# Splitting the experts' second weights during the first network instead of during the experts' first pass

## The chip, the cores and the metric

The kernel runs on one core of a Trainium2 chip. The metric is the time of one execution on the device in microseconds (us), taken as the median of several executions; lower is better. A change of 0.2% (2.4 us) is about what a measurement of this kernel can tell from no change.

## The reference

Everything is float32. A linear attention over 2304 tokens is followed by a network with a gated activation (the first network), and that by four experts whose outputs are mixed by probabilities:

```
kv  = einsum('bhsd,bhde->bhse', q, einsum('bhsd,bhse->bhde', k, v))
x   = kv / sqrt(mean(kv*kv) + 1e-6) * g_norm            # (2304, 512)
h   = x @ w_in                                          # w_in (512, 2048)
x   = (h * clip(h + 3, 0, 6) / 6) @ w_out               # w_out (2048, 512)
p   = probs / (sum(probs) + 1e-9)                       # (2304, 4)
out = sum over e of p[:, e] * (relu(x @ w1[e]) @ w2[e]) # w1 (4, 512, 1024), w2 (4, 1024, 512)
```

## The kernel before

Every float32 operand of a matrix product is split into a rounded high part and a low remainder, and a product is three TensorE matmuls (high by high, high by low, low by high). A split is one ScalarE copy (the high part) and one VectorE subtraction (the low part); the helper `split` at L667 and L668 records both.

**Stages.** Attention takes the first 90 us or so. The first network then runs over "items" (u, t, f): 16 hidden tiles of 128 columns in five units u, five token blocks t (four of 512 tokens and one of 256), tile f within the unit. `step(n)` issues the first layer of item n (`ff_in`: 12 matmuls into one of two PSUM banks `ph`), the second layer of item n-3 (`ff_out`: 12 matmuls into `po`), and pieces of `convert`, which loads and splits the weights of a later hidden tile. Between the layers stand ScalarE L371, VectorE L372 (the last reader of `ph`), ScalarE L374 and VectorE L375. When a unit is complete, VectorE L411 adds `po` to `acc`.

**The experts.** Three passes of 768 tokens. An expert's hidden columns are taken 256 at a time, which makes 16 "quads" k. In the first pass `quad(k)` makes seven block products of Strassen's kind with `product` (L821, 6 matmuls each, in turn into the PSUM banks `qa` and `qb`) and brings the results out with ScalarE and VectorE (L856 is ScalarE's copy `us` of the second product; the product that follows two places later writes the same bank). `outs(k-1)` then multiplies by the second weights (L777, 36 matmuls). Beside the matmuls the first pass prepares the weights of the next quads: `convert_in` splits w1 and its block sums into `win` and stores them (L687), `convert_out` splits w2 into `wout`, forms four block differences of w2 on GpSimd (L699, tile `tw`), splits them, and stores the differences and three plain blocks to DRAM (`dtw`, L709 and L711). Passes two and three read `dtw` and the stored `win` back and use Strassen's form for both layers (L1029).

**Order.** Inside the attention the order is written by hand. Behind it a scheduler sets the order on each engine when the program is built; an engine then takes its instructions in that order. All large DMAs are issued by SyncE (SP), which also issues in order and stands still at a DMA whose source or target is not ready.

**Buffers the change touches.** `cvp` holds the four 2 KB-per-partition work tiles of `convert` (x, a and two r), `rawp` three raw weight tiles of 4 KB; both pools end after the first network, and their space is used again by `win`. `tw` lived in `accp`, whose five buffers hold `acc` until the tokens of a pass have been read.

Of the kernel before, what the change touches and what calls it, by code (L numbers as in the profile page):

```python
# [8 lines left out]
F32 = mybir.dt.float32  # L9
F32R = mybir.dt.float32r  # L10
U32 = mybir.dt.uint32
AF = mybir.ActivationFunctionType
ALU = mybir.AluOpType
# [4 lines left out]
def kernel(  # L18
# [18 lines left out]
    nc = tc.nc  # L37
    B, H, S, D = q.shape
    NT, DM = out.shape
    E = moe2_w1.shape[0]  # L40
    P = 128
# [17 lines left out]
    FP = NF2 // 2  # L59
    NW = 8  # L60
    NA = NW - 2
    LAG = 3
    RATE = (4200, 3000, 2600, 2900, 0)
    FMAX = 3.0e38
    PADL, PADR = 232, 248
# [6 lines left out]
    accp = ctx.enter_context(tc.tile_pool(name="accp", bufs=NB))  # L72
# [7 lines left out]
    cvp = early.enter_context(tc.tile_pool(name="cvp", bufs=1, side="right"))  # L80
    rawp = early.enter_context(tc.tile_pool(name="rawp", bufs=3, side="right"))
# [3 lines left out]
    dram = ctx.enter_context(tc.tile_pool(name="dram", bufs=1, space=bass.MemoryType.DRAM))  # L85
    psk = attps.enter_context(tc.tile_pool(name="psk", bufs=1, space=bass.MemoryType.PSUM))
    psp = attps.enter_context(tc.tile_pool(name="psp", bufs=1, space=bass.MemoryType.PSUM))
    NG = CJ * 2
# [25 lines left out]
    ftiles = [(u, f) for u in range(NUNIT) for f in range(UF[u])]  # L114
# [38 lines left out]
    def convert(n):  # L153

        u, f = ftiles[n]
        W[u, f] = w = wp.tile([P, 2, 2, KD * P], F32R, tag=f"w{(NA + n) % NW}", name="w")

        for h in range(2):
            lo, hi = raw[n, h][:, :, 0], raw[n, h][:, :, 1]
            x = cvp.tile([P, KD * P], U32, tag="x", name="x")  # L160
            a = cvp.tile([P, KD * P], U32, tag="a", name="a")
            r = cvp.tile([P, KD * P], F32, tag="r", bufs=2, name="r")
            xf, up = x.bitcast(F32), r.bitcast(U32)
            nc.scalar.activation(out=xf, in_=hi.bitcast(F32), func=AF.Abs)
            nc.scalar.activation(out=up, in_=lo, func=AF.Copy, scale=2.0 ** -29)
            yield 0
            nc.vector.tensor_scalar(
                out=xf, in0=xf, scalar1=2.0 ** -15, scalar2=122880.0, op0=ALU.max, op1=ALU.min)
            yield 335
            nc.vector.tensor_scalar(  # L170
                out=x, in0=x, scalar1=5, scalar2=2,
                op0=ALU.logical_shift_left, op1=ALU.logical_shift_right)
            yield 335
            nc.vector.scalar_tensor_tensor(
                out=a, in0=hi, scalar=0xC0000000, in1=x, op0=ALU.bitwise_and, op1=ALU.bitwise_or)
            yield 600
            e = nc.gpsimd if POOLED[0] <= (n, h) < POOLED[1] else nc.vector
            e.tensor_tensor(out=up, in0=up, in1=a, op=ALU.add)
            yield 600 if e is nc.vector else 0
            nc.scalar.activation(out=w[:, h, 0], in_=r, func=AF.Copy)  # L180
            yield 0
            nc.vector.tensor_tensor(out=w[:, h, 1], in0=r, in1=w[:, h, 0].bitcast(F32), op=ALU.subtract)
            if n:
                load_raw()
            yield 600

# [312 lines left out]
    with tc.manual_schedule(engines=engines):  # L499
# [103 lines left out]
        for y in range(2):  # L603
            h = half[y]
            for jp in range(2):
# [5 lines left out]
                out=prob[h, B * HH:], in0=dp[h, y::2, CJ - 1],  # L611
                in1=psum_e[h, y::2, CJ - 1:].to_broadcast([D, 2, E]), op=ALU.mult)

    N3 = start[NU1 - 1, 0] + 3 * UF[NU1 - 1]
    for n in range(NB, N3 + 1):
        step(n)
    assert cv[0] == len(ftiles)

# [18 lines left out]
    quads = [(0, e, j) for e in range(E) for j in range(FP)]  # L639
    NQ = len(quads)  # L640
    SIDES = NPASS - 1
    TC = DM // 2
    dwin = [dram.tile([P, 2, 7, 2, P], F32, name=f"dwin{k}") for k in range(NQ)]
    dtw = [dram.tile([P, 7, 2, 2, TC], F32, name=f"dtw{g}") for g in range(NQ // 2)]
    dwo = [dram.tile([P, 2, 2, DM], F32, name=f"dwo{k}") for k in range(2)]
    raw2, win, wout, xs, g2, acc2 = {}, {}, {}, {}, {}, {}
    sums = xsp.tile([P, 4, 2, P], F32, tag="sums", name="sums")
    st1 = xsp.tile([P, 2, TH], F32, tag="st1", name="st1")
# [16 lines left out]
    def split(dst, src):  # L665

        nc.scalar.activation(out=dst[0], in_=src, func=AF.Copy)  # L667
        nc.vector.tensor_tensor(out=dst[1], in0=src, in1=dst[0].bitcast(F32), op=ALU.subtract)  # L668
# [21 lines left out]
    def convert_out(k):  # L690

        r = raw2.pop(k)[:, 1].rearrange("p (f d) -> p f d", f=2)
        wout[k] = w = wp.tile(
            [P, 2, 2, DM], F32R, tag=f"w{(NA + len(ftiles) + 2 + k % 2) % NW}", name="wout")
        b11, b12, b21, b22 = (r[:, f, c * TC:(c + 1) * TC] for f in range(2) for c in range(2))
        tw = accp.tile([P, 2, 4, TC], F32R, tag="acc", name="tw")
        ts = tw[:, 1].bitcast(F32)
        for z, a, b in ((0, b12, b11), (1, b22, ts[:, 0]), (2, b22, b12), (3, b21, ts[:, 1])):
            nc.gpsimd.tensor_tensor(out=ts[:, z], in0=a, in1=b, op=ALU.subtract)  # L699
        for f in range(2):  # L700
            split([w[:, f, y] for y in range(2)], r[:, f])
            yield
        for z in (slice(0, 2), slice(2, 4)):
            split([tw[:, y, z] for y in range(2)], ts[:, z])
            if z.start:
                load2(k + 2)
                dt = dtw[k // 2][:, :, k % 2]
                for z, m in enumerate((4, 2, 3, 5)):
                    nc.sync.dma_start(out=dt[:, m], in_=tw[:, :, z].bitcast(F32))  # L709
                for m, f, c in ((0, 0, 0), (1, 1, 0), (6, 1, 1)):  # L710
                    nc.sync.dma_start(out=dt[:, m], in_=w[:, f, :, c * TC:(c + 1) * TC].bitcast(F32))  # L711
                if k >= NQ - 2:
                    nc.sync.dma_start(out=dwo[k - NQ + 2], in_=w.bitcast(F32))
            yield

    def build(p):
# [160 lines left out]
    def run(g):  # L877
        return lambda: next(g, None)
# [24 lines left out]
    for k in range(NQ):  # L903
        last_of_pass = k + 1 == NQ
        ci, co = convert_in(k + 1) if 0 < k and k + 1 < NQ else iter(()), convert_out(k)
        side = rest_in + builds + [run(co)] * 4 + [run(ci)] * (1 if builds else 5)
        rest_in = [run(ci)] * 4 if builds else []
        builds = []
        if last_of_pass:
            nxt = build(1)  # L910
            side += [nxt[1], nxt[0]]
            builds = [nxt[m] for m in (6, 5, 2, 7, 3, 4)]
        seed()
        every = -(-NI2 * 6 // len(side))
        for z, _ in enumerate(filler):
            if z % every == every - 1 and side:
                side.pop(0)()
        for x in side:
            x()
        quad(k)  # L920
        if k + 1 < NQ:
            seed = first_product(k + 1)
        filler = outs(k)
# [16 lines left out]
    def load_t(n):  # L940
        if 2 * n >= 7 * (NG2 - 1):
            return
        tt[n] = t = accp.tile([P, 2, 2, 2, TC], F32R, tag="acc", name="tt")
        for y in range(2):
            g, m = divmod(2 * n + y, 7)
            if g < NG2 - 1:
                nc.sync.dma_start(out=t[:, y].bitcast(F32), in_=dtw[g % (NQ // 2)][:, m])

    def front(g, jj):

# [190 lines left out]
```

## Time and profile before

| | |
|---|---|
| median of 3 runs | 1207.6 us (1207.46 to 1207.98) |
| profiled execution, its own time | 1207.61 us |
| its span, first to last instruction | 1205.8 us |
| TensorE busy | 1182.4 us of the span |
| mean granted TensorE clock | 0.997 |

The span is 1.8 us shorter than the time of the same execution. A matmul's end is modelled in the profile, so places where TensorE stands still are found as idle time with what ended it, and as the distance between the starts of equal pieces of work.

### The profile page before, as it was taken

The page shows a single profiled execution, that of the slowest core. Times are in us where ns is not written, and L with a number is a line of the kernel's source. Part 1 is how long each engine was busy: PE and PEld are TensorE (multiplying, and loading weights), DVE is VectorE, ACT ScalarE, POOL GpSimd, SP SyncE. Part 2 cuts the span into 40 slices and gives each one's busy share as a digit, 9 for nine tenths or more (in the row PEclk, how much of TensorE's full clock was granted, in tenths as well). Part 3 has the DMA queues.
Part 4 walks back from the last instruction along what each step waited for, and adds up shares of the span by engine and source line. Part 5 has one row for each costly group of instructions (what it writes and reads, how often), then busy time and mean ns, then how long its engine had stood idle before and what let it go on. Part 6 is the DMA issues. An engine that isn't in the chain of part 4 may idle for free.

```text
span 1205.8 us, 19484 instructions
## 1 busy us (share of the span) xinstructions
PE 1182.4 (98%) x7810; PEld 1076.4 (89%) x7810; DVE 766.1 (64%) x1380; ACT 561.2 (47%) x1020; POOL 55.8 (5%) x79
## 2 busy tenths in 40 slices
PE   8999999999999999999999999999999999999998
PEld 7788888888888889888888889999999999999997
DVE  5889994833433765565757565666666866666663
ACT  6876553522322445455555434444444544444442
POOL 1100000000000022211111000000000000000000
PEclk9999999999999999999999999999999999999999
DMA  9723330200200237788888866667666887666641
GB/s 319 230 87 105 103 107 2 86 1 1 71 1 1 123 97 247 286 291 303 282 281 283 336 235 230 250 245 249 245 249 244 300 279 266 241 253 246 248 171 53
DMA packets 87278, 230.45 MB, mean 191 GB/s; under 512 B 7188, under 2 KB 52244, under 8 KB 80532
## 3 DMA queue, kind: packets, MB, share of 16 engines
q1 hardware_dynamic: 86704, 228.43, 53.8%
q8 instruction: 61, 1.00, 0.3%
q10 hardware_dynamic: 484, 0.79, 0.2%
q14 instruction: 29, 0.24, 0.1%
HBM read 163.65 MB, written 65.54 MB: 190 GB/s over the span
## 4 chain that ended last, share of the span: by engine, by line
PE 73%; DVE 8%; ACT 7%; DMA 6%; POOL 2%; issue 2%; SPq 2%; POOLq 0%; DVEq 0%; ACTq 0%
PE slot L1029 16%; PE po L393 14%; PE qb L821 11%; PE qa L821 10%; PE ph L358 5%; PE ph L360 5%; PE ph L359 5%; PE po L777 4%; DMA dtw<-tw 3%; POOL tw L699 2%; ACT so L667 2%; DMA dwin<-win 1%; PE slot L1106 1%; ACT ar L958 1%; DVE sums L1006 1%
## 5 line engine op out<-in xcount | busy, mean ns | idle before, releaser
L1029 PE MATMUL slot<-tt,so 128*128 128x256 f32 x1890 | 248.6, 283 | 3.0 <-ACT so L667 1.4
L1029 PEld LDWEIGHTS slot<-tt,so 128*128 128x128 f32 x1890 | 240.3, 190 | 7.0 <-ACT slot L1037 4.6
L821 PE MATMUL qb<-xs,win 128*128 128x384 f32 x1008 | 204.4, 337 | 4.8 <-ACT us L856 3.8
L821 PE MATMUL qa<-xs,win 128*128 128x384 f32 x1008 | 204.7, 337 | 3.9 <-ACT us L856 3.0
L393 PE MATMUL po<-gH,w 128*128 128x512 f32 (+1 forms) x632 | 191.6, 368 | 0.6 <-DVE acc L411 0.3
L821 PEld LDWEIGHTS qb<-xs,win 128*128 128x128 f32 x1008 | 177.1, 189 | 8.1 <-ACT us L856 6.1
L821 PEld LDWEIGHTS qa<-xs,win 128*128 128x128 f32 x1008 | 173.1, 189 | 6.8 <-ACT us L856 4.4
L794 DVE SCALAR_TENSOR_TENSOR acc<-slot,prob,acc 128x256 f32<-128x256 f32 (+1 forms) x252 | 108.1, 484 | 106.4 <-PE slot L1029 96.5
L393 PEld LDWEIGHTS po<-gH,w 128*128 128x128 f32 x632 | 115.8, 188 | 21.1 <-DVE acc L411 0.8
L777 PE MATMUL po<-wout,g 128*128 128x512 f32 x576 | 133.8, 390 | 0.0
L777 PEld LDWEIGHTS po<-wout,g 128*128 128x128 f32 x576 | 107.9, 188 | 21.9
L358 PE MATMUL ph<-xh,w 128*128 128x512 f32 (+1 forms) x320 | 118.6, 371 | 0.0
L359 PE MATMUL ph<-xl,w 128*128 128x512 f32 (+1 forms) x320 | 117.9, 368 | 0.0
L360 PE MATMUL ph<-xh,w 128*128 128x512 f32 (+1 forms) x320 | 117.8, 368 | 0.0
L371 ACT ACTIVATE r<-ph,three 128x512 f32<-128x512 f32 (+1 forms) x80 | 51.3, 641 | 141.3 <-PE ph L360 140.4
L372 DVE SCALAR_TENSOR_TENSOR r<-r,ph 128x512 f32<-128x512 f32 (+1 forms) x80 | 50.5, 632 | 104.6 <-ACT r L371 104.6
L393 PE MATMUL po<-gL,w 128*128 128x512 f32 (+1 forms) x316 | 116.4, 368 | 0.0
L668 DVE TENSOR_TENSOR so<-ar,so 128x768 fp32r<-128x768 f32 x94 | 89.4, 952 | 36.5 <-ACT so L667 36.4
L667 ACT ACTIVATE so<-ar 128x768 fp32r<-128x768 f32 x94 | 79.3, 844 | 38.1 <-PE slot L1029 33.5
L958 ACT ACTIVATE ar<-cs 128x384 f32<-128x384 f32 x64 | 33.4, 521 | 80.9 <-DVE cs L987 48.2
L358 PEld LDWEIGHTS ph<-xh,w 128*128 128x128 f32 x320 | 60.3, 188 | 10.7 <-DVE r L372 0.4
L360 PEld LDWEIGHTS ph<-xh,w 128*128 128x128 f32 x320 | 60.3, 188 | 10.1
(160 smaller groups left out, 1335.3 us busy)
## 6 DMA issues: line engine op xcount, KB each, us to landing
win<-dwin SPq DMA_DIRECT2D x32, 1792.0 KB, 8.1
tt<-dtw SPq DMA_DIRECT2D x105, 512.0 KB, 5.8
dwin<-win SPq DMA_DIRECT2D x16, 1792.0 KB, 6.4
raw<-in_moe_w_dram SPq DMA_DIRECT2D x32, 512.0 KB, 4.8
dtw<-tw SPq DMA_DIRECT2D x64, 256.0 KB, 6.0
dtw<-wout SPq DMA_DIRECT2D x48, 256.0 KB, 6.0
raw<-in_moe_w_in_dram SPq DMA_DIRECT2D x14, 512.0 KB, 3.7
raw<-in_moe_w_out_dram SPq DMA_DIRECT2D x14, 512.0 KB, 3.7
```

Source lines behind the costliest of these rows:

```text
L358: nc.tensor.matmul(ph, lhsT=w[:, 0, c, :], rhs=xH[t][:, c, :], start=(c == 0), stop=False)
L359: nc.tensor.matmul(ph, lhsT=w[:, 0, c, :], rhs=xL[t][:, c, :], start=False, stop=False)
L360: nc.tensor.matmul(ph, lhsT=w[:, 1, c, :], rhs=xH[t][:, c, :], start=False, stop=(c == KD - 1))
L371: lambda: nc.scalar.activation(out=r, in_=ph, func=AF.Relu, bias=three[:, 0:1]),
L372: lambda: nc.vector.scalar_tensor_tensor(out=r, in0=r, scalar=6.0, in1=ph, op0=ALU.min, op1=ALU.mult),
L393: nc.tensor.matmul(po_t[u, t][o], lhsT=lhsT, rhs=rhs, start=(f == 0 and m == 0), stop=(f == UF[u] - 1 and m == 2))
L667: nc.scalar.activation(out=dst[0], in_=src, func=AF.Copy)
L668: nc.vector.tensor_tensor(out=dst[1], in0=src, in1=dst[0].bitcast(F32), op=ALU.subtract)
L777: nc.tensor.matmul(ps[i], lhsT=lhsT, rhs=w[:, f, y], start=(j == 0 and f == 0 and m == 0), stop=(j == FP - 1 and f == 1 and m == 2))
L794: nc.vector.scalar_tensor_tensor(out=acc2[i][:, c], in0=ps, scalar=pe, in1=acc2[i][:, c], op0=ALU.mult, op1=ALU.add)
L821: nc.tensor.matmul(bank, lhsT=w[:, wy, AOP[m], c], rhs=xs[m][:, xy, c], start=first and n == 0, stop=n == 5, skip_group_check=True)
L1029: nc.tensor.matmul(dst, lhsT=o[:, sy_, jj, i * P:(i + 1) * P], rhs=t[:, jj, ty], start=fresh and m == 0 and i != 1, stop=m == 5, skip_grou ...
```

## The change

The formation of the block differences and the whole of `dtw` and `dwo` (the plain w2 of the last two quads, read by the very last group) move out of `convert_out` into a new generator `blocks`, which runs during the first network. It loads w2 a second time into `rawp` (L626 of the new file, 512 KB a quad), forms the differences on VectorE (L654 to L659; GpSimd has no part in it any more), splits differences and plain blocks with ScalarE (L644) and VectorE (L645) into the four `cvp` tiles, and stores high and low parts apart (L648, L650). It runs in two stretches, quads 0 to 7 and quads 8 to 15, called from `second(n)` after `step(n)`. For that the conversion of the last two hidden tiles of the first network is held back: their raw tiles are loaded only at n = 48 and 49. `convert_out` keeps the two splits of `wout` and the load of the quad after next. The order of the seven blocks in `dtw` is another one, and the reader follows it.

```
+    HELD = 13
@@ convert
-            if n:
+            if n and n != HELD:
                 load_raw()
@@ new, behind the attention and ahead of the loop over step(n)
+    def load_rawt(k):
+        e, j = experts[k]
+        f = 2 * j * P
+        rawt[k] = r = rawp.tile([P, 2, DM], F32, tag="raw", name="rawt")
+        nc.sync.dma_start(out=r, in_=moe2_w2[e, f:f + 2 * P, :].rearrange("(f p) d -> p f d", p=P))
+    def blocks(k, end, deep):
+        r = rawt[k].rearrange("p f (c d) -> p (f c) d", c=2)
+        last = k - 2 * NG + 2
+        def new():
+            tag = ("x", "a", "r", "r")[turns[0] % 4]
+            turns[0] += 1
+            return cvp.tile([P, 2, TC], F32R, tag=tag, bufs=2 if tag == "r" else 1, name="tb")
+        def keep(m, src, low, n=2):
+            high = new()
+            low = low if low is not None else new()
+            src = low.bitcast(F32) if src is None else src
+            nc.scalar.activation(out=high[:, :n], in_=src, func=AF.Copy)
+            nc.vector.tensor_tensor(out=low[:, :n], in0=src, in1=high[:, :n].bitcast(F32), op=ALU.subtract)
+            for y, x in ((0, high), (1, low)):
+                c = min(n, 7 - m) if m else 1
+                nc.sync.dma_start(out=dtw[k // 2][:, m:m + c, k % 2, y], in_=x[:, :c].bitcast(F32))
+                if last >= 0 and m < 2:
+                    nc.sync.dma_start(
+                        out=dwo[last][:, int(m > 0), y].rearrange("p (c d) -> p c d", c=2), in_=x.bitcast(F32))
+        odd = new()
+        nc.vector.tensor_tensor(out=odd.bitcast(F32), in0=r[:, 1::2], in1=r[:, 0:2], op=ALU.subtract)
+        yield
+        even = new()
+        ev = even.bitcast(F32)
+        nc.vector.tensor_tensor(out=ev[:, 0], in0=r[:, 3], in1=odd[:, 0].bitcast(F32), op=ALU.subtract)
+        nc.vector.tensor_tensor(out=ev[:, 1], in0=r[:, 2], in1=ev[:, 0], op=ALU.subtract)
+        yield
+        keep(3, None, odd)
+        yield
+        keep(5, None, even)
+        yield
+        keep(1, r[:, 2:4], None)
+        yield
+        if last >= 0:
+            keep(0, r[:, 0:2], None)
+        else:
+            keep(0, r[:, 0:1], None, 1)
+        rawt.pop(k)
+        if k + deep < end:
+            load_rawt(k + deep)
+        yield
+    def second(n):
+        if n == 37:
+            for k in range(2):
+                load_rawt(k)
+            stream.extend(x for k in range(NG) for x in [blocks(k, NG, 2)] * 6)
+        elif n == 54:
+            for k in range(NG, NG + 3):
+                load_rawt(k)
+            stream.extend(x for k in range(NG, 2 * NG) for x in [blocks(k, 2 * NG, 3)] * 6)
+        for _ in range(5 if 37 < n < 48 else 4 if 54 < n < 68 else 0):
+            if stream:
+                next(stream.pop(0))
+        if n in (48, 49):
+            load_raw()
     for n in range(NB, N3 + 1):
         step(n)
+        second(n)
@@ convert_out
-        tw = accp.tile([P, 2, 4, TC], F32R, tag="acc", name="tw")
-        ts = tw[:, 1].bitcast(F32)
-        for z, a, b in ((0, b12, b11), (1, b22, ts[:, 0]), (2, b22, b12), (3, b21, ts[:, 1])):
-            nc.gpsimd.tensor_tensor(out=ts[:, z], in0=a, in1=b, op=ALU.subtract)
         for f in range(2):
             split([w[:, f, y] for y in range(2)], r[:, f])
-            yield
-        for z in (slice(0, 2), slice(2, 4)):
-            split([tw[:, y, z] for y in range(2)], ts[:, z])
-            if z.start:
+            if f == 1:
                 load2(k + 2)
-                dt = dtw[k // 2][:, :, k % 2]
-                for z, m in enumerate((4, 2, 3, 5)):
-                    nc.sync.dma_start(out=dt[:, m], in_=tw[:, :, z].bitcast(F32))
-                for m, f, c in ((0, 0, 0), (1, 1, 0), (6, 1, 1)):
-                    nc.sync.dma_start(out=dt[:, m], in_=w[:, f, :, c * TC:(c + 1) * TC].bitcast(F32))
-                if k >= NQ - 2:
-                    nc.sync.dma_start(out=dwo[k - NQ + 2], in_=w.bitcast(F32))
             yield
@@ the loop over quads
-        side = rest_in + builds + [run(co)] * 4 + [run(ci)] * (1 if builds else 5)
+        side = rest_in + builds + [run(co)] * 2 + [run(ci)] * (1 if builds else 5)
@@ load_t, passes two and three
-                nc.sync.dma_start(out=t[:, y].bitcast(F32), in_=dtw[g % (NQ // 2)][:, m])
+                nc.sync.dma_start(out=t[:, y].bitcast(F32), in_=dtw[g % NG][:, (0, 1, 5, 4, 3, 6, 2)[m]])
```

TensorE's order is the same in both programs, matmul for matmul. The order moves at three places on the engines beside it.

First, ScalarE in the experts' first pass, at the end of quad 2's products and the beginning of quad 3's; `raw_4831` is the raw tile of quad 4. Before:

```order
L833 ACTIVATE qb<-qa 128x384
L667 ACTIVATE win<-sums 128x512 x2
L667 ACTIVATE tw<-tw 128x512 x2
L667 ACTIVATE wout<-raw_4831 128x512 x2
L856 ACTIVATE us<-qa 128x384
```

The same place now, where `raw_5258` is the raw tile of quad 4:

```order
L897 ACTIVATE qa<-qb 128x384
L746 ACTIVATE win<-sums 128x512 x2
L746 ACTIVATE wout<-raw_5258 128x512 x2
L920 ACTIVATE us<-qa 128x384
L922 ACTIVATE sums<-qb 128x384
```

The two copies of `tw` ahead of `wout` and `us` are gone, and nothing has come in their place.

Second, VectorE in the first stretch, at items 41 and 42 of the first network (each begins with the instruction that reads `ph`). Before:

```order
L372 SCALAR_TENSOR_TENSOR r<-r,ph 128x512
L375 TENSOR_TENSOR gL<-r,gH 128x512
L372 SCALAR_TENSOR_TENSOR r<-r,ph 128x512
L375 TENSOR_TENSOR gL<-r,gH 128x512
```

The same two items now:

```order
L373 SCALAR_TENSOR_TENSOR r<-r,ph 128x512
L376 TENSOR_TENSOR gL<-r,gH 128x512
L658 TENSOR_TENSOR tb<-rawt,tb 128x256
L659 TENSOR_TENSOR tb<-rawt,tb 128x256
L645 TENSOR_TENSOR tb<-tb 128x512 x2
L373 SCALAR_TENSOR_TENSOR r<-r,ph 128x512
L645 TENSOR_TENSOR tb<-rawt,tb 128x256
L376 TENSOR_TENSOR gL<-r,gH 128x512
L645 TENSOR_TENSOR tb<-rawt,tb 128x512
L654 TENSOR_TENSOR tb<-rawt 128x512
L658 TENSOR_TENSOR tb<-rawt,tb 128x256
```

One quad's blocks are spread over two items, and they stand between the two instructions that each item needs.

Third, VectorE at items 49 and 50, between the stretches, where the held hidden tiles are converted. Before:

```order
L372 SCALAR_TENSOR_TENSOR r<-r,ph 128x256
L375 TENSOR_TENSOR gL<-r,gH 128x256
L182 TENSOR_TENSOR w<-r,w 128x512 x2
L178 ISA r<-r,a 128x1024
L174 SCALAR_TENSOR_TENSOR a<-raw,x 128x512
L178 ISA r<-r,a 128x1024
L372 SCALAR_TENSOR_TENSOR r<-r,ph 128x512
L182 TENSOR_TENSOR w<-r,w 128x512 x2
L375 TENSOR_TENSOR gL<-r,gH 128x512
```

The same two items now:

```order
L373 SCALAR_TENSOR_TENSOR r<-r,ph 128x256
L376 TENSOR_TENSOR gL<-r,gH 128x256
L168 TENSOR_SCALAR x<-x 128x512
L171 TENSOR_SCALAR x<-x 128x512
L175 SCALAR_TENSOR_TENSOR a<-raw,x 128x512
L179 ISA r<-r,a 128x1024
L373 SCALAR_TENSOR_TENSOR r<-r,ph 128x512
L168 TENSOR_SCALAR x<-x 128x512
L183 TENSOR_TENSOR w<-r,w 128x512
L171 TENSOR_SCALAR x<-x 128x512
L376 TENSOR_TENSOR gL<-r,gH 128x512
L175 SCALAR_TENSOR_TENSOR a<-raw,x 128x512
```

Most of this conversion was done by item 36 before; now all of it stands at items 49 to 53, and the first blocks of the second stretch follow at item 53.

## Rows read from the trace of the kernel before

**Rows 1.** Page, parts 1 and 2: busy time; DMA share in 40 slices.
```profile
PE 1182.4 (98%) x7810; PEld 1076.4 (89%) x7810; DVE 766.1 (64%) x1380; ACT 561.2 (47%) x1020; POOL 55.8 (5%) x79
...
DMA  9723330200200237788888866667666887666641
```
**Rows 2.** Windows: stretch, length, then busy us of each engine, clock, DMA share, GB/s.
```profile
90.00:420.00 330.00, 329.98 (x1556) 277.08 (x1555) 206.56 (x373) 134.71 (x224) 0.00 (x0) 1.00 0.17 54
241.00:256.00 15.00, 15.00 (x68) 12.43 (x67) 4.15 (x6) 3.48 (x6) 0.00 (x0) 1.00 0.00 1
440.00:710.00 270.00, 262.22 (x1337) 235.75 (x1336) 165.46 (x311) 139.53 (x278) 42.43 (x58) 0.99 0.78 274
492.50:495.90 3.40, 3.40 (x11) 3.40 (x12) 1.37 (x3) 1.27 (x3) 0.00 (x0) 0.50 0.75 221
```
**Rows 3.** Waits, all engines, 430 to 730 us: total, times, longest.
```profile
POOL tw L699 <- DMA dtw<-tw: 145.8, 11, 19.2
...
ACT win L667 <- DVE sums L680: 11.5, 13, 1.1
...
PE qb L821 <- ACT us L856: 3.8, 4, 2.1
...
PE qa L821 <- ACT us L856: 3.0, 3, 1.8
```
**Rows 4.** Timeline of ScalarE, 472 to 512 us: start, length, instruction, idle before.
```profile
489.51 0.63 ACT L667 ACTIVATE tw<-tw 128x512 fp32r<-128x512 f32 x1 [6.39 <-POOL tw L699]
...
491.91 0.47 ACT L856 ACTIVATE us<-qb 128x384 f32<-128x384 f32 x1
...
507.73 1.15 ACT L667 ACTIVATE wout<-raw 128x512 fp32r<-128x512 f32 x2 [0.88 <-PE po L777]
508.79 0.49 ACT L856 ACTIVATE us<-qa 128x384 f32<-128x384 f32 x1
```
**Rows 5.** Timeline of GpSimd, 440 to 560 us.
```profile
487.35 1.43 POOL L699 TENSOR_TENSOR tw<-raw 128x256 f32<-128x256 f32 x2 [19.25 <-DMA dtw<-tw]
```
**Rows 6.** Timeline of TensorE, 463 to 716 us: starts of the blocks of `outs`.
```profile
464.28 8.36 PE L777 MATMUL po<-wout,g 128*128 128x512 f32 x36
479.82 8.36 PE L777 MATMUL po<-wout,g 128*128 128x512 f32 x36
...
693.39 8.36 PE L777 MATMUL po<-wout,g 128*128 128x512 f32 x36
```
**Rows 7.** Tile `tw`: instructions with ns min/median/max, and its stores' us to landing.
```profile
L667 ACT ACTIVATE tw<-tw x32: 616/632/636, 432.3 to 670.4; 128x512 fp32r<-128x512 f32 x32
L668 DVE TENSOR_TENSOR tw<-tw x32: 683/692/694, 433.1 to 671.1; 128x512 fp32r<-128x512 f32 x32
...
DMA to landing us min/median/max: 2.1/6.0/8.3
```
**Rows 8.** Groups by form, 90 to 440 us: busy us, mean ns, idle before.
```profile
L371 ACT ACTIVATE r<-ph,three 128x512 f32<-128x512 f32 x59 | 40.5, 686 | 118.5 <-PE ph L360 117.6 <-DVE w L182 0.8
...
L375 DVE TENSOR_TENSOR gL<-r,gH 128x256 fp32r<-128x256 f32 x11 | 4.6, 421 | 2.9 <-ACT gH L374 2.9
L374 ACT ACTIVATE gH<-r 128x256 fp32r<-128x256 f32 x11 | 4.6, 418 | 5.7 <-DVE r L372 5.7
```
**Rows 9.** Chain that ended last, 240 to 300 us: start, length, blocks of `ff_out`.
```profile
240.41 2.72 PE po L393 x12
245.85 2.72 PE po L393 x12
...
288.09 2.75 PE po L393 x12
292.27 2.75 PE po L393 x12
```
**Rows 10.** Page, part 6: DMAs, count, KB each, median us to landing.
```profile
dtw<-tw SPq DMA_DIRECT2D x64, 256.0 KB, 6.0
...
raw<-in_moe_w_in_dram SPq DMA_DIRECT2D x14, 512.0 KB, 3.7
```

More of the change, by code (lines that the diff above doesn't have):

```diff
@@ L612 @@
                 in1=psum_e[h, y::2, CJ - 1:].to_broadcast([D, 2, E]), op=ALU.mult)
+    TC = DM // 2
+    experts = [(e, j) for e in range(E) for j in range(FP)]
+    NG = len(experts) // 2
+    dtw = [dram.tile([P, 7, 2, 2, TC], F32, name=f"dtw{g}") for g in range(NG)]
+    dwo = [dram.tile([P, 2, 2, DM], F32, name=f"dwo{k}") for k in range(2)]
+    rawt = {}
+    def load_rawt(k):
[3 more added lines that the diff above has]
+        nc.sync.dma_start(out=r, in_=moe2_w2[e, f:f + 2 * P, :].rearrange("(f p) d -> p f d", p=P))
@@ new lines @@
+    turns = [0]
+    def blocks(k, end, deep):
[39 more added lines that the diff above has]
+        yield
@@ new lines @@
+    stream = []
+    def second(n):
+        if n == 37:
+            assert todo[0] == (HELD + 1, 1) and cv[0] == HELD + 1
+            for k in range(2):
+                load_rawt(k)
+            stream.extend(x for k in range(NG) for x in [blocks(k, NG, 2)] * 6)
+        elif n == 54:
+            assert not stream and cv[0] == len(ftiles)
+            for k in range(NG, NG + 3):
[6 more added lines that the diff above has]
+            load_raw()
@@ L616 @@
         step(n)
-    assert cv[0] == len(ftiles)
+        second(n)
+    assert not stream
     early.close()
@@ L641 @@
     SIDES = NPASS - 1
-    TC = DM // 2
     dwin = [dram.tile([P, 2, 7, 2, P], F32, name=f"dwin{k}") for k in range(NQ)]
-    dtw = [dram.tile([P, 7, 2, 2, TC], F32, name=f"dtw{g}") for g in range(NQ // 2)]
-    dwo = [dram.tile([P, 2, 2, DM], F32, name=f"dwo{k}") for k in range(2)]
     raw2, win, wout, xs, g2, acc2 = {}, {}, {}, {}, {}, {}
@@ L694, in convert_out @@
             [P, 2, 2, DM], F32R, tag=f"w{(NA + len(ftiles) + 2 + k % 2) % NW}", name="wout")
-        b11, b12, b21, b22 = (r[:, f, c * TC:(c + 1) * TC] for f in range(2) for c in range(2))
-        tw = accp.tile([P, 2, 4, TC], F32R, tag="acc", name="tw")
-        ts = tw[:, 1].bitcast(F32)
-        for z, a, b in ((0, b12, b11), (1, b22, ts[:, 0]), (2, b22, b12), (3, b21, ts[:, 1])):
-            nc.gpsimd.tensor_tensor(out=ts[:, z], in0=a, in1=b, op=ALU.subtract)
         for f in range(2):
             split([w[:, f, y] for y in range(2)], r[:, f])
-            yield
-        for z in (slice(0, 2), slice(2, 4)):
-            split([tw[:, y, z] for y in range(2)], ts[:, z])
-            if z.start:
+            if f == 1:
                 load2(k + 2)
-                dt = dtw[k // 2][:, :, k % 2]
-                for z, m in enumerate((4, 2, 3, 5)):
-                    nc.sync.dma_start(out=dt[:, m], in_=tw[:, :, z].bitcast(F32))
-                for m, f, c in ((0, 0, 0), (1, 1, 0), (6, 1, 1)):
-                    nc.sync.dma_start(out=dt[:, m], in_=w[:, f, :, c * TC:(c + 1) * TC].bitcast(F32))
-                if k >= NQ - 2:
-                    nc.sync.dma_start(out=dwo[k - NQ + 2], in_=w.bitcast(F32))
             yield
```

## The prediction

> **What bounds the kernel now.** I read the page first: TensorE is busy 1182.4 of 1205.8 us [rows 1], so only its idle time and its slow stretches can be won. Then the windows, for the two stages that the change touches [rows 2]. In the first network TensorE works 329.98 of 330 us; nothing can be won there, only lost. VectorE works 206.6 us of these and ScalarE 134.7, but in 241 to 256 us, where no weights are converted, they work 4.15 and 3.48 of 15 us and DMA does nothing. In the first expert pass TensorE works 262.2 of 270 us at clock 0.99, so 7.8 us are idle, and DMA is busy at 0.78 with 274 GB/s.
>
> The waits say who ends that idle time: TensorE's two largest entries are products that wait for ScalarE's copy `us`, 3.8 us in 4 places and 3.0 in 3, longest 2.1 [rows 3]. ScalarE is busy about half of the stretch, so I followed one such place back in the timelines. `us` starts at 491.91 us, behind a copy of `tw` at 489.51 that had waited 6.39 us for GpSimd [rows 4]; GpSimd's subtraction at 487.35 had stood 19.25 us until a store of the `tw` before it had landed [rows 5]. Such waits for stores add up to 145.8 us [rows 3], a store taking 6.0 us at the median [rows 7]. So the chain is store, GpSimd, ScalarE in its fixed order, TensorE. Behind the stall the granted clock is 0.50 for 3.4 us (1.2 instead of 2.4 GHz) [rows 2], half of which, 1.7 us, is lost.
>
> **What the change removes.** The chain as a whole: ScalarE's order has no `tw` left ahead of `us`, and nothing waits on GpSimd. What a quad takes without the chain I read from the starts of the `outs` blocks: 464.28 to 479.82 is 15.54 us, a quad without a stall. From 464.28 to 693.39 are 14 quads in 229.11 us, where 14 times 15.54 makes 217.56. The difference, **11.55 us** [rows 6], holds idle time and slow clock together, and it is the term of the gain. Are 15.54 us within reach of every quad? At 507.73 a quad without a stall already shows the order that all will have: `wout` starts when TensorE's `outs` ends, and `us` follows at 508.79 [rows 4], which TensorE did not have to wait for. The 32 copies of `tw` on ScalarE (0.632 us, 20.2 in all) and 32 subtractions on VectorE (0.692 us, 22.1) [rows 7] also go; they lie beside matmuls, and as work they count nothing.
>
> **What it adds, and what hides it.** A quad's blocks cost VectorE four instructions of 0.69 us and three 256-wide ones of 0.42 us, together 4.0 us, and ScalarE three of 0.63 and one of 0.42, 2.3 us (512-wide forms as in [rows 7], 256-wide as in [rows 8]). For 16 quads that is 64 us of VectorE and 37 us of ScalarE. By the order a quad is spread over two items; an item of 512 tokens takes 245.85 - 240.41 = 5.44 us, and a short one 292.27 - 288.09 = 4.18 us [rows 9]. So VectorE gets 4.0 us more in 10.88 us, on top of 4.15 in 15 us: under 0.7 busy. In sum this fits; what matters is whether an instruction that waits holds up the two that each item needs, since both engines work in order.
>
> Slack of these two: `ph` has two banks, so the VectorE instruction that empties it may end as late as the first layer of the item after next, three blocks of 2.72 us on. Less ScalarE's copy and VectorE's own instruction (0.69 each) [rows 8], some 6.8 us are left; where two of the three blocks are 256 wide, 1.43 us each (4.18 - 2.75), 5.6 - 1.4 = some 4 us.
>
> Now the wait. A block tile is formed, its low part split, stored, written again as another block's high part, stored again, once per quad. That loop is 0.69 + 0.63 + 0.69 + 0.63 = 2.64 us and two stores. No row shows such a store on idle queues; its bounds are the 2.1 us minimum and the 6.0 us median among the crowd of the first pass [rows 7]. With 2.1 the loop is 6.9 us, well inside 10.88, and the added cost is **0**. With 6.0 it is 14.6 us, 3.8 more than two items allow: 16 quads fall 60 us behind, of which each of the two stretches absorbs its slack of 6.8, and some **47 us** are lost. It decides at a store of (10.88 - 2.64) / 2 = 4.1 us. I take a value near the lower bound: the network moves 54 GB/s now [rows 2], and the change adds, per two items, 8 stores of 256 KB and a load of 512 KB, 2.6 MB in 10.88 us or 240 GB/s, below the 274 of the first pass, in single pairs of stores and not in the seven at once that `tw` was followed by. A 512 KB load took 3.7 us where the network loads now [rows 10], and that is twice a store's size.
>
> ScalarE and VectorE take their instructions in order, as `us` at 491.91 shows, which did not pass the copies in front of it [rows 4]. The Trainium skill, "TensorE: Matmul & The Clock Gate", section "Architectural detail: the array is 16× 32×32, not 1× 128×128", says that these two engines' queues are strictly first in, first out; by that rule a late store holds the network's own instructions too, which is the slower rival below. The Trainium skill, "DMA: Bandwidth & Descriptors", section "Anatomy of one DMA — SWDGE (gpsimd) path", gives some 2.0 us fixed plus the bytes at 436 GB/s; that is 2.6 us for 256 KB, for a path that this kernel's stores do not take, and the loop would be 7.8 us: also inside two items, and the sum stays. No row settles it, since the fastest store of this trace took 2.1 us.
>
> The held conversion: items 46 to 52 last 6 x 4.18 + 5.44 = 30.5 us, and at items 49 to 53 VectorE has four half tiles to convert, five instructions each, beside its own work and L411. Counted from the order that is nearly all of the 30 us, so VectorE can fall 2 to 3 us behind there; slack is 4 to 6.8 us. I put it at 0, with 3 as the upper bound. The same goes for the end, where the last quad's blocks meet the preparation of the experts (items 67 on): 0, at most 3. Stores of the pass move to where DMA is idle; the first pass loses 112 stores, and what loads remain can only come sooner. Passes two and three keep their work and reads.
>
> **Sum.** 1207.6 - 11.6 + 0 = **1196.0 us**; the profiled execution's own time is 1207.61, that of the runs too, so nothing is to be converted.
>
> **The rivals.**
> *A part is eaten.* Either the network stalls 3 to 6 us (the two upper bounds just named), or in the first pass another wait takes the chain's place. For the second speaks that ScalarE already waits 11.5 us in 13 places for `sums` [rows 3], which is in front of `wout` and `us` in the order now; 0.4 us at each of 15 quads would be 6 us. Against it speaks the quad at 507.73, which has that order and no stall. 1198.5 to 1205.2 us.
> *It moves nothing.* The stall costs as much at another place: the gain of 11.6 us is matched by as much in the network, as when a store takes (11.6 + 13.6) / 32 = 0.8 us more than the deciding 4.1. Within 2.4 us of before, 1205.2 to 1210 us.
> *Slower.* Stores land in more than 5.0 us on the mean: TensorE waits in 270 to 400 us on `ph` or on gH and gL, each quad costs up to 3.8 us, and each stall also brings 1.2 GHz behind it, as at 492.5. Up to 47 us: 1210 to 1243. For it speaks the 6.0 us median, against it the idle queues (slices 9 to 14 of the DMA line, 241 to 422 us, read 002002 [rows 1]).
>
> **How the numbers follow.** The forecast, 1193.5 to 1198.5, gets 0.66; a part eaten, up to 1205.2, 0.16; nothing moved 0.07; slower 0.11. A measurement tells about 0.2%, 2.4 us, from no change. So faster is 0.82, same 0.07, slower 0.11. The range has to leave out 2 in 10 at most: from 1193.5 (a little of the quad ahead of 464 us and of the load on DMA may also be won) to 1205.0 it holds the first two cases.
>
> **What would show it.** Right: in the first pass no product waits for `us`, the `outs` blocks start 15.5 us apart throughout, and the clock stays at 1.0; GpSimd is idle; in 260 to 400 us VectorE is busy about 0.7 or more, TensorE still without a gap, and block stores land in 2 to 4 us. Wrong in size: the blocks are 15.9 us apart, or products wait for `us` behind `wout` or `sums`. Wrong in sign: ScalarE's copies of blocks wait for DMA, and first-layer matmuls wait for L372 (now L373), or the second stretch's items come late on their `w`.

## The result and the profile after

The changed kernel takes 1195.99 us (median of 4 runs, 1194.90 to 1198.16) against 1207.66 us, a ratio of 0.9905 (95% interval 0.9888 to 0.9923). That is 11.7 us faster; the forecast was 1196.0 us. The profiled execution took 1195.82 us with a span of 1194.0 us.

The page of the changed kernel, parts 1 and 2, answers to [rows 1]:

```profile
PE 1177.2 (99%) x7810; PEld 1074.5 (90%) x7810; DVE 801.4 (67%) x1460; ACT 577.9 (48%) x1052; POOL 7.6 (1%) x15
...
DMA  8723240566766624444444466667666887666641
```

The span falls by 11.8 us, TensorE's busy time by 5.2: matmuls at half clock, as in the last of [rows 2], count there with their full length, and so does a wait that hides behind a matmul's modelled end; 6.6 us were idle time. The DMA line shows the move: slices 8 to 14 read 5667666 where 2002002 stood, and slices 16 to 23 read 4 where 7 or 8 stood.

The windows of the changed kernel, columns as in [rows 2]:

```profile
90.00:420.00 330.00, 329.05 (x1551) 275.97 (x1550) 261.46 (x482) 168.09 (x288) 0.00 (x0) 1.00 0.52 170
241.00:256.00 15.00, 15.00 (x67) 12.39 (x67) 8.76 (x17) 6.50 (x12) 0.00 (x0) 1.00 0.74 238
440.00:710.00 270.00, 269.19 (x1397) 245.09 (x1397) 157.14 (x298) 127.20 (x254) 0.00 (x0) 1.00 0.45 172
```

In the first pass TensorE's idle time is 0.8 us instead of 7.8, at clock 1.00. In the network VectorE is busy 8.76 of 15 us where it was 4.15, and TensorE still works all 15. Over the 330 us of the first line it stands 0.95 us, where it stood 0.02 before.

The timeline of TensorE, starts of the `outs` blocks in the changed kernel, answers to [rows 6]:

```profile
464.29 8.36 PE L841 MATMUL po<-wout,g 128*128 128x512 f32 x36
...
681.59 8.36 PE L841 MATMUL po<-wout,g 128*128 128x512 f32 x36
```

Between these two lie 14 quads in 217.30 us, 15.52 each, where before they took 229.11. The pass thus gives 11.81 us, and the span's whole gain is 11.8: up to 464 us the two programs stand within 0.01 us of each other, and passes two and three take equally long.

That the first 464 us agree so closely is partly chance: the changed kernel stood 0.92 us at 320.64 us in the network, the kernel before 0.31 and 0.23 us at 444.60 and 451.38 us, and executions differ by more than that before the pass (the first block starts at 463.72 us in remove_only and at 465.69 in pass_stores, neither of them with idle time in the network).

The waits of the changed kernel, 430 to 730 us (total, times, longest), answer to [rows 3]; below them the tile of the blocks, `tb` (ns min/median/max, first and last start):

```profile
ACT wout L746 <- PE po L841: 71.1, 14, 5.1
...
ACT win L746 <- DVE sums L759: 11.6, 14, 0.8
...
PE qb L885 <- ACT qb L1026: 0.8, 1, 0.8
```

```profile
L644 ACT ACTIVATE tb<-tb x32: 612/632/635, 224.6 to 395.7; 128x512 fp32r<-128x512 f32 x32
L645 DVE TENSOR_TENSOR tb<-tb x32: 680/684/694, 226.5 to 396.9; 128x512 fp32r<-128x512 f32 x32
...
  DMA dtw<-tb: 37.3, 39
...
DMA to landing us min/median/max: 1.7/2.3/4.6
```

No product waits for `us`. ScalarE now waits for TensorE in front of `wout`, 71.1 us, which is spare time and no loss. A block store lands after 2.3 us at the median, and the block instructions waited 37.3 us for stores without a wait of TensorE for them.

### The profile page after: what moved, and what is told of

It reads as the page before. It is cut to its first block, busy times and chain, and to the rows that moved or that the text cites. A ratio compares the mean times of both kernels' runs of the same rounds, so it can differ in the third digit from the quotient of the medians.

```text
span 1194.0 us, 19613 instructions
## 1 busy us (share of the span) xinstructions
PE 1177.2 (99%) x7810; PEld 1074.5 (90%) x7810; DVE 801.4 (67%) x1460; ACT 577.9 (48%) x1052; POOL 7.6 (1%) x15
## 4 chain that ended last, share of the span: by engine, by line
PE 80%; DVE 8%; ACT 6%; DMA 5%; issue 1%; DVEq 0%; SPq 0%; ACTq 0%
PE slot L1093 16%; PE qa L885 13%; PE qb L885 13%; PE po L394 12%; PE po L841 10%; PE ph L359 4%; PE ph L361 4%; PE ph L360 4%; DMA dtw<-tb 2%; ACT so L746 2%; PE slot L1170 1%; ACT ar L1022 1%; DVE sums L1070 1%; ACT slot L1101 1%; DMA qin<-in_q_dram 1%
## 5 line engine op out<-in xcount | busy, mean ns | idle before, releaser
L373 DVE SCALAR_TENSOR_TENSOR r<-r,ph 128x512 f32<-128x512 f32 (+1 forms) x80 | 50.3, 629 | 37.3 <-ACT r L372 37.2
```

The costliest lines, as they stand in the source:

```text
L373: lambda: nc.vector.scalar_tensor_tensor(out=r, in0=r, scalar=6.0, in1=ph, op0=ALU.min, op1=ALU.mult),
```

## The experiments

### The two halves of the change, apart

**add_only** keeps the network of the changed kernel and puts the old first pass behind it, which stores into the spare tensors `dtx`:

```diff
+        for z, a, b in ((0, b12, b11), (1, b22, ts[:, 0]), (2, b22, b12), (3, b21, ts[:, 1])):
+            nc.gpsimd.tensor_tensor(out=ts[:, z], in0=a, in1=b, op=ALU.subtract)
...
+                dt = dtx[k // 2][:, :, k % 2]
```

> The change's addition alone: the blocks are formed, split and stored in the first network as in the changed kernel, and the first expert pass forms, splits and stores them a second time as before (into spare DRAM that nothing reads). Theory (the work in the network is hidden, the gain comes from the first pass alone): 1207.6 to 1209 us, TensorE in 240 to 420 us idle 1 us at most, and the waits of products for us about 7 us as before. Rival (the addition costs some us, which a larger gain in the first pass hides in the whole change): 1210 us or more, with idle time in 240 to 420 us.

Measured: 1208.95 us, ratio to before 1.0006 (0.9991 to 1.0020). Its windows:

```profile
240.00:420.00 180.00, 180.00 (x840) 150.66 (x839) 136.00 (x248) 87.86 (x153) 0.00 (x0) 1.00 0.68 228
440.00:710.00 270.00, 261.25 (x1337) 235.34 (x1336) 163.12 (x307) 137.52 (x274) 43.85 (x60) 0.99 0.78 274
```

The network with all block work in it has no idle time on TensorE; the first pass is much as in [rows 2], 8.75 us idle against 7.78. The addition costs nothing that can be measured.

**remove_only** keeps the first pass of the changed kernel and stores raw weights from the network:

```diff
-            nc.scalar.activation(out=high[:, :n], in_=src, func=AF.Copy)
-            nc.vector.tensor_tensor(out=low[:, :n], in0=src, in1=high[:, :n].bitcast(F32), op=ALU.subtract)
+            for y in range(2):
...
+                nc.sync.dma_start(out=dtw[k // 2][:, m:m + c, k % 2, y], in_=src[:, :c])
```

> The change's removal alone: the first pass is that of the changed kernel; in the network the second weights are loaded and stored as they are, with no formation and no split (the blocks that passes two and three read are therefore raw weights). Theory: 1195 to 1196 us, at most the 0.9 us of idle time at 320 us better than the change. Rival (VectorE and ScalarE work in the network costs more than that idle time shows): 1193.5 us or less.

Measured: 1194.45 us, ratio 0.9883 (0.9866 to 0.9899). The whole gain, and 0.7 to 1.5 us less than the two medians of the changed kernel (1195.99, and 1195.18 in a later comparison, below). The time lies between the two expectations, 0.55 us under the theory's and 0.95 over the rival's. By these medians the work of ScalarE and VectorE in the network costs 0.7 to 1.5 us, which is within the noise.

**half** forms quads 0 to 7 in the network and leaves 8 to 15 in the first pass:

```diff
-        for _ in range(5 if 37 < n < 48 else 4 if 54 < n < 68 else 0):
+        for _ in range(5 if 37 < n < 48 else 0):
...
+        if k < NG:
...
+            return
+        tw = accp.tile([P, 2, 4, TC], F32R, tag="acc", name="tw")
```

> The change for quads 0 to 7 only: their blocks in the network's first stretch, those of quads 8 to 15 in the first pass as before; there is no second stretch. Theory: outs blocks are 15.5 us apart in the first half of the pass and show the stalls of before in the second; of the excess of 11.6 us in before, 6.4 us lie up to 596.5 us (132.26 us for 8 quads, against 124.2) or a little less, and about 5 us stay: 1199.5 to 1203 us. Rival (the second stretch in the network costs what it gains there, or the first does): the time is that of the change, or that of before.

Measured: 1203.11 us, ratio 0.9960 (0.9947 to 0.9974). Its `outs` blocks:

```profile
463.72 8.36 PE L858 MATMUL po<-wout,g 128*128 128x512 f32 x36
...
572.37 8.36 PE L858 MATMUL po<-wout,g 128*128 128x512 f32 x36
...
688.88 8.36 PE L858 MATMUL po<-wout,g 128*128 128x512 f32 x36
```

Seven quads without the forming take 108.65 us, 15.52 each; the next seven, with it, 116.51, which is 7.9 too many. The time follows the place of the forming. The size was off: I had put some 5 us there, and the time is 0.1 us above the range.

### What in the first pass cost the time

**tw_free** takes away the link at which the prediction's chain began, the store of `tw`:

```diff
-                    nc.sync.dma_start(out=dt[:, m], in_=tw[:, :, z].bitcast(F32))
+                    nc.sync.dma_start(out=dt[:, m], in_=w[:, z % 2, :, z // 2 * TC:(z // 2 + 1) * TC].bitcast(F32))
```

> The kernel before, with the four stores of block differences of a quad taken from wout instead of tw, at the same size and number (passes two and three read plain blocks in their place); tw is free as soon as it is split, and its copies stay in ScalarE's order in front of us. Theory (the chain begins at the store of tw): GpSimd no longer waits for a DMA, most of 11.6 us are won, 1195.5 to 1199 us. Rival (the copies as such are too much for ScalarE ahead of us, or the traffic is the cost): 1203 us or more with products still waiting for us.

Measured: 1221.03 us, ratio 1.0102 (1.0085 to 1.0118): slower than before, a clear miss. Its waits, 430 to 730 us:

```profile
POOL tw L699 <- DMA raw<-in_moe_w_dram: 168.6, 12, 19.0
ACT tw L667 <- POOL tw L699: 74.2, 31, 7.7
...
PE qa L821 <- DVE cs L864: 8.0, 3, 3.2
...
PE qb L821 <- ACT us L856: 5.2, 3, 2.3
```

GpSimd no longer waits for stores, 145.8 us in [rows 3]; it waits 168.6 us for the load of the raw weights instead. ScalarE waits as long for `tw` as before, 74.2 us against 72.1 in the same view of the kernel before. The last releaser has been exchanged and the next one stood right behind it. The timelines suggest a loop, which no run tested apart: SP issues the loads behind the first store from `wout` (508.31 us, the loads at 508.95 and 510.08), GpSimd starts at 519.39, ScalarE copies `tw` at 521.56 and the next `wout` only behind it, at 523.96. Why this is 13 us worse than the kernel before stays open.

**tw_pool** leaves store and buffer and takes `tw` out of ScalarE's and VectorE's order:

```diff
-            split([tw[:, y, z] for y in range(2)], ts[:, z])
+            nc.gpsimd.tensor_copy(out=tw[:, 0, z], in_=ts[:, z])
+            nc.gpsimd.tensor_tensor(out=tw[:, 1, z], in0=ts[:, z], in1=tw[:, 0, z].bitcast(F32), op=ALU.subtract)
```

> The kernel before, with the split of tw (high copy and low part) done by GpSimd instead of ScalarE and VectorE; the subtractions, all stores and the one buffer of tw stay in the first pass. Theory (TensorE stood still only because copies of tw wait in ScalarE's order in front of us): the wait for stores stays on GpSimd, where nobody queues behind it, no product waits for us, and the time is 1195.5 to 1198 us. Rival (the stores themselves, their traffic or SyncE's order held by them, cost the time): little changes, 1203 us or more, and later loads of weights or of win come late.

Measured: 1220.22 us, ratio 1.0100 (1.0083 to 1.0117): the theory is missed; the time is on the rival's side of the bound, but far from its "little changes". Its waits, 430 to 730 us, of SP's queue first, then of the engines:

```profile
SPq L710 <- POOL tw L705: 185.9, 20, 20.3
```

```profile
DVE sums L678 <- DMA raw<-in_moe_w_dram: 20.3, 10, 2.9
...
PE qa L822 <- DVE cs L865: 7.7, 5, 2.4
PE qb L822 <- DVE cs L865: 7.7, 4, 2.4
```

No product waits for `us`, so that link was real. But SP stands 185.9 us at stores whose `tw` is not ready, with the loads of raw weights behind them in its order; VectorE then waits for those loads with `sums`, and `cs` behind it in its order holds the products for 15.4 us. GpSimd also holds up VectorE itself (last section): in 440 to 710 us a subtraction for `wout` took VectorE 1.04 us at the mean instead of 0.69, and so did one for `win` from `sums`. How the loss divides between the two was not taken apart. In the kernel before no instruction for `sums` took more than 0.43 us and `wout` took 0.69, so its stalls show no sign of this.

**pass_form** and **pass_stores** then split the removed work itself: forming without stores, stores without forming. The first has the network of remove_only.

```diff
 pass_form: in the first pass
-                    nc.sync.dma_start(out=dt[:, m], in_=tw[:, :, z].bitcast(F32))
-                    nc.sync.dma_start(out=dt[:, m], in_=w[:, f, :, c * TC:(c + 1) * TC].bitcast(F32))
 pass_stores: against the kernel before
-            nc.gpsimd.tensor_tensor(out=ts[:, z], in0=a, in1=b, op=ALU.subtract)
-            split([tw[:, y, z] for y in range(2)], ts[:, z])
-                    nc.sync.dma_start(out=dt[:, m], in_=tw[:, :, z].bitcast(F32))
+                    nc.sync.dma_start(out=dt[:, m], in_=w[:, z % 2, :, z // 2 * TC:(z // 2 + 1) * TC].bitcast(F32))
```

> The first pass of the kernel before without its stores of blocks: tw is formed and split there as before, and not stored; the network stores raw weights in place of blocks, as in the run of the removal alone (passes two and three read these). Theory after the two misses (a load of raw weights held behind late stores in SyncE's order, or a store of tw, must make tw late; without the stores neither is): the forming itself is free, 1194.5 to 1198 us, and no product waits for us. Rival (ScalarE's two tw copies in front of us are too much by themselves, or GpSimd waits for raw loads all the same): 1202 us or more, with GpSimd waiting for DMA of raw and products for us.

> The kernel before without the forming of tw: nothing is subtracted on GpSimd or split for it; the first pass still makes seven block stores a quad, all from wout (plain blocks in place of differences). Theory (the traffic and SyncE's order alone do not stop TensorE; it takes a tw in ScalarE's or GpSimd's order that waits for them): 1194.5 to 1199 us. Rival (late loads behind the stores make VectorE's sums for win late, and cs behind them, as in the run with the split on GpSimd): 1202 us or more, with products waiting for VectorE's cs.

| first pass | forming | no forming |
|---|---|---|
| with stores | before: 1208.08 us | pass_stores: 1195.86, ratio 0.9907 (0.9891 to 0.9923) |
| without stores | pass_form: 1204.12, ratio 0.9967 (0.9954 to 0.9980) | changed kernel again: 1195.18, ratio 0.9901 (0.9884 to 0.9918) |

All four were timed on the same chip. The stores alone cost 0.7 us, within the noise, at 291 GB/s where the pass moved 274 before [rows 2]; the window of pass_stores:

```profile
440.00:710.00 270.00, 269.19 (x1399) 245.03 (x1399) 156.70 (x297) 126.67 (x252) 0.00 (x0) 1.00 0.82 291
```

The forming alone costs about 9 us (1204.12 - 1195.18), against the theory that I held by then. The networks of these two differ; against remove_only, which has the network of pass_form, it is 9.7. Waits of pass_form, 430 to 730 us, and VectorE's timeline around one of its stalls:

```profile
POOL tw L759 <- DMA raw<-in_moe_w_dram: 87.8, 7, 13.5
ACT tw L727 <- POOL tw L759: 50.1, 32, 3.5
...
PE qa L874 <- DVE cs L917: 2.9, 3, 1.3
PE qb L874 <- ACT us L909: 2.6, 1, 2.6
```

```profile
577.18 0.42 DVE L740 TENSOR_TENSOR sums<-sums,raw 128x256 f32<-128x256 f32 x1
577.51 0.96 DVE L741 TENSOR_TENSOR sums<-raw 128x256 f32<-128x256 f32 x1
578.40 0.95 DVE L743 TENSOR_TENSOR sums<-raw,sums 128x256 f32<-128x256 f32 x1
580.80 0.69 DVE L728 TENSOR_TENSOR tw<-tw 128x512 fp32r<-128x512 f32 x1 [1.45 <-POOL tw L759]
...
583.80 4.04 DVE L847 SCALAR_TENSOR_TENSOR acc<-po,prob,acc 128x512 f32<-128x512 f32 x6
587.75 1.28 DVE L728 TENSOR_TENSOR wout<-raw,wout 128x512 fp32r<-128x512 f32 x2
...
589.88 0.55 DVE L917 TENSOR_TENSOR cs<-qa,us 128x384 f32<-128x384 f32 x1
```

At an expert's last quad VectorE has six additions to the result (4.04 us) besides. `tw` comes late from GpSimd, the additions start at 583.80, and `cs` at 589.88 is late for TensorE, which stands 1.26 us there; three such places and one at `us` (2.6 us, at 460.97, ahead of the first `outs` block) make the idle time of that execution. Without stores `tw` waits for its raw weights, and for GpSimd's 3 us behind them.

### How near its limit the network is

**stores_x2** and **stores_x4** issue each block store two and four times (`dtx` is one or three spare tensors):

```diff
                 nc.sync.dma_start(out=dtw[k // 2][:, m:m + c, k % 2, y], in_=x[:, :c].bitcast(F32))
+                for dx in dtx:
+                    nc.sync.dma_start(out=dx[k // 2][:, m:m + c, k % 2, y], in_=x[:, :c].bitcast(F32))
```

> The changed kernel, with every block store of the network issued twice (the second into spare DRAM). Theory: the tile of a block comes free later, 3 to 4 us instead of 2.3, still under the 4.1 us at which the loop of one tile no longer fits two items: 1196 to 1198 us, TensorE in 240 to 420 us idle 2 us at most. Rival (the network is already at its limit): 1200 us or more.

> The changed kernel, with every block store of the network issued four times (three of them into spare DRAM), so 32 stores of 256 KB a quad or 8.4 MB in two items of 10.88 us, some 770 GB/s, more than any stretch of the trace moved. Theory: stores take well over 4.1 us, the loop of one tile paces the network, and the time is far above, 1250 us or more, with first-layer products waiting for VectorE's L373 and ScalarE's copies of blocks waiting for DMA. Rival (ScalarE and VectorE get past late stores, or stores land as fast as alone): under 1215 us.

Measured: 1203.55 us, ratio 0.9963 (0.9947 to 0.9979), and 1359.08 us, ratio 1.1258 (1.1237 to 1.1278). Of the doubled stores the window and TensorE's only wait in it, then TensorE's waits with four:

```profile
240.00:420.00 180.00, 175.45 (x804) 145.49 (x803) 120.53 (x219) 79.93 (x137) 0.00 (x0) 0.98 0.95 315
```

```profile
PE ph L359 <- ACT w L181: 4.5, 1, 4.5
```

```profile
PE ph L359 <- ACT w L181: 82.2, 2, 80.9
PE qb L965 <- ACT win L749: 63.4, 1, 63.4
```

The landing of the stores of `tb`, with two and with four:

```profile
DMA to landing us min/median/max: 2.0/3.0/5.4
```

```profile
DMA to landing us min/median/max: 1.8/3.5/6.2
```

At the median a store landed in 3.0 us with two and 3.5 with four, below the mean of 4.1 us at which I had put the limit; yet doubling cost 7 to 8 us, a miss: the 4.5 us at `w`, and half clock behind them (the granted clock was 0.91 in 300 to 340 us). With four the time is as expected, the place of the wait is not.

The DMA share points to the reason: 0.95 at 315 GB/s. A quad stores seven times 256 KB (two of the prediction's eight stores are of 128 KB); twice that and a load of 512 KB are 4.2 MB in 10.88 us, or 385 GB/s, more than was moved (with four, 351 GB/s in 330 to 420 us). In the first stretch a quad took 13.2 us (7 quads from 224.18 to 316.58 us) where it takes 10.4 in the changed kernel (223.84 to 296.68). SP's issuing is not the limit: 16 stores took it 7.3 us (0.44 and 0.47 each at the median). That the limit is throughput is read from the share; the loop of one tile, whose stores also queue behind one another, was not tested apart from it.

And TensorE does not stand at `ph` or gH and gL: it stands for `w`, the held hidden tiles, whose conversion comes behind the first stretch in the order; SP issued their last three loads 23 to 25 us later than in the changed kernel (at 318.9, 330.0 and 331.7 us). The changed kernel, at 0.67 of DMA in 240 to 420 us, has less than a factor of two to spare.

### A version without the last 0.9 us

TensorE's one idle time in the network, 0.92 us at 320.64 in the profiled execution, waits for VectorE's L412 (the addition to `acc`), which stands among the instructions of the held conversion, where VectorE has hardly a gap. **pool_add** gives one step of that conversion to GpSimd, **pool_low** another; **after_again** is the changed kernel once more. The wait, in the changed kernel, 90 to 430 us:

```profile
PE po L394 <- DVE acc L412: 0.9, 1, 0.9
```

```diff
 pool_add
-            e = nc.gpsimd if POOLED[0] <= (n, h) < POOLED[1] else nc.vector
+            e = nc.gpsimd if POOLED[0] <= (n, h) < POOLED[1] or n > HELD else nc.vector
 pool_low
-            nc.vector.tensor_tensor(out=w[:, h, 1], in0=r, in1=w[:, h, 0].bitcast(F32), op=ALU.subtract)
+            (nc.gpsimd if n > HELD else nc.vector).tensor_tensor(out=w[:, h, 1], ...)
```

> The changed kernel, with the addition in the conversion of the two held hidden tiles (four instructions of 0.69 us on VectorE between 306 and 322 us) given to GpSimd. Theory (the one idle time of 0.92 us of TensorE in the network, at 320.6 us, comes from VectorE being full there): the idle time goes, 1195 us, 0 to 1 us better than the change. Rival (GpSimd is slower at it and the converted tile then comes late): idle time there of 1 us or more, 1196.5 us or more.

> The changed kernel, with the four low-part subtractions at the end of the held conversion given to GpSimd (2.8 us less for VectorE between 306 and 322 us, and nothing in the middle of the conversion waits for GpSimd). Theory (VectorE is full there, and L412 is late by it): the idle time of 0.9 us at 320 us goes, 0 to 1.3 us better than the changed kernel of the same call. Rival (the low parts come late for the first product with them, or the execution's spread is larger than the gain): no difference or slower.

> The changed kernel once more, for comparison on the same chip: 1194.9 to 1198.2 us as measured. Theory: idle time at 320 us of 0.9 us again. Rival (that idle time was an accident of one execution): none there.

Measured: pool_add 1197.29 us, ratio 0.9919 (0.9900 to 0.9938); pool_low 1199.32, ratio 0.9934 (0.9920 to 0.9948); after_again 1195.18, ratio 0.9901 (0.9884 to 0.9918), which answers for the changed kernel beside pool_low. TensorE's wait at that place in pool_low, and the window of after_again:

```profile
PE po L394 <- DVE acc L412: 2.6, 1, 2.6
```

```profile
240.00:420.00 180.00, 180.00 (x840) 150.89 (x840) 136.57 (x248) 88.64 (x153) 0.00 (x0) 1.00 0.67 227
```

Both versions made the wait longer (1.5 us in pool_add). pool_low is 4.1 us slower than after_again on the same chip; pool_add, timed on another, cannot be told from the changed kernel. The changed kernel itself has no idle time there in the second profile. The wait comes and goes between executions: add_only has none either, half has 0.60 us at 320.05. No version beat the changed kernel.

## Why the prediction was right

**The gain.** The term of 11.55 us, read from the starts of equal blocks, was 11.81, and all 14 quads became as short as the first had been (15.51 to 15.54 us). Reading the distance between blocks was the better measure by more than the prediction says: the waits (3.8 and 3.0 us) and the half clock (1.7 us) make 8.5 only. The rest does not show as idle time of the matmuls; the weight loads ahead of them waited longer for `us` in the kernel before, 10.5 us (430 to 730 us):

```profile
PEld qb L821 <- ACT us L856: 6.1, 7, 2.5
PEld qa L821 <- ACT us L856: 4.4, 4, 2.1
```

That forecast and median agree within 0.01 us is chance: the runs of the changed kernel spread over 3.3 us.

**The cover.** VectorE and ScalarE's work in the network was priced at 0, and add_only and remove_only show 0 to 1.5 us. The store of 2.1 us at the lower bound was 2.3. The held conversion, put at 0 with 3 as bound, was 0.92 in one profile and 0 in another. Of the rivals, ScalarE still waits 11.6 us for `sums`, and no product waits because of it.

**Three steps of the working were wrong, though the sum was not.** First, "the chain is store, GpSimd, ScalarE in its fixed order, TensorE" was read as one chain with the store at its head. The links from GpSimd on are borne out: taking `tw` out of the first pass, with all stores left in (pass_stores), gives the whole gain. The head was read rightly as what ended GpSimd's waits, but the time did not hang on it: without stores of `tw` (tw_free) the raw loads stepped in its place and the time rose by 13 us. What fits all four corners of the table is that stores only make a forming later that is late anyway: 9 us without them, 12 to 13 with. And the copies and subtractions of `tw`, of which the prediction says that "as work they count nothing", do count by their place in the order: at an expert's last quad in pass_form VectorE's additions and `cs` come late behind them. Had the change only freed `tw` of its stores or given it another engine, this reading would have forecast a gain where two runs lost 12 and 13 us; it came out because the change removes the chain as a whole.

Second, the price at which the slower rival decides. "It decides at a store of" 4.1 us took the landing time as the price of more traffic. With twice the stores the median landing time was 3.0 us and 7 to 8 us were lost, with DMA 0.95 busy, and at the held weights instead of at `ph`. The traffic added was also put too high: with two of the eight stores at half size it is 2.4 MB a quad, 217 GB/s over 10.88 us, and 226 were measured in 240 to 420 us, where a quad took 10.4.

Third, in the slower rival, "each stall also brings 1.2 GHz behind it". In the kernel before, one of the seven stalls at `us` did: behind the stalls of 1.04 and 1.82 us at 526.37 and 608.83 us the granted clock was 1.00. The forecast did not use this.

**Not settled:** why forming and storing together cost some 3 us more than the sum of both, why tw_free is slower than the kernel before, how tw_pool's loss divides between late loads and VectorE's longer instructions, and how much of the 9 us of pass_form is VectorE held up by GpSimd (last section). Whether a second buffer for `tw` would have helped was not tried.

## What to carry to other kernels

A wait names the last releaser only: before a fix of that link is priced, ask what the waiting work would wait for next, since here the next one was worse. Work that stands in an in-order queue ahead of what the bound engine needs was worth taking out of that stretch whole here, into one where TensorE is full and the other engines and DMA are not; taking out one link was not. The room in such a stretch showed in the DMA share and in what stands behind the moved work in order, not in the landing time of one transfer.

## What the runs showed of the hardware that was not expected

VectorE can stand still while GpSimd works. Timelines of pool_low, VectorE and then GpSimd:

```profile
310.32 1.41 DVE L171 TENSOR_SCALAR x<-x 128x512 uint32<-128x512 uint32 x1
...
314.14 0.43 DVE L171 TENSOR_SCALAR x<-x 128x512 uint32<-128x512 uint32 x1
```

```profile
310.15 1.29 POOL L183 TENSOR_TENSOR w<-r,w 128x512 fp32r<-128x512 f32 x1 [254.35 <-ACT w L181]
```

The same instruction takes 0.43 us alone and 1.41 us when it starts behind GpSimd's, ending 0.3 us after it: it all but stood until GpSimd had done. So moving 0.69 us off VectorE cost it about 1 us at three of the four places, and the four together cost it 3.0 us where 2.8 were moved. At the fourth, VectorE had three additions to `acc` in its order, which read one input from PSUM; they took 1.08 us together beside GpSimd, no longer than alone. In pass_form the subtractions for `sums` take 0.96 instead of 0.42 in the same way (its timeline above; GpSimd works from 577.46 us on). The Trainium skill, "SBUF — State Buffer", section "Who interferes with whom", says that the two engines share one pair of ports as an exclusive lock; these rows agree.
